# Multiplying by Z inside the recurrence for one unit, with heads kept on their row half, merged masks, diagonals on ScalarE and a new instruction order

## The chip, the cores and the metric

The kernel runs on one core of a Trainium2 chip, in float32. The metric is the device time of one launch in microseconds (us). Engines are named as the profile does: PE is TensorE's matmul, PEld its weight load, DVE is VectorE, ACT ScalarE, POOL GpSimd, SP SyncE. Before the change the median of three runs is 597.41 us (595.88 to 597.56).

## The reference

```python
# attention: B, H, S, D = 4, 8, 768, 48
k_n = k / (np.linalg.norm(k, axis=-1, keepdims=True) + 1e-06)
for t in range(S):
    y[:, :, t] = np.einsum('bhd,bhde->bhe', q[:, :, t], state)
    v_old = np.einsum('bhde,bhd->bhe', state, kt)
    state = state + bt * np.einsum('bhd,bhe->bhde', kt, vt - v_old)
# mixer: x is (4, 768, 384), U (768, 32), V (32, 768), w_ch1 (384, 1536), w_ch2 (1536, 384)
h = x.transpose(0, 2, 1) @ U @ V
u = x + h.transpose(0, 2, 1)
out = u + np.maximum(u @ w_ch1, 0.0) @ w_ch2
```

A delta-rule recurrence runs over 768 tokens for each of 32 pairs of batch and head. Its output goes, heads side by side, through a low-rank mixing of tokens and a two-layer network over channels.

## The kernel before

The recurrence is computed in chunks of 64 tokens. Within a chunk the sequential part is a triangular system, so the kernel forms the products of the keys with themselves, inverts a unit triangular matrix (called Z in what follows) and from then on needs only matmuls. A *unit* is half of one batch element: six chunks of all eight heads. There are eight units, two (n = 0, 1 for the first) per batch element b.

The eight heads stand on 128 partitions as two row halves of 64 (g), and within each half four heads, numbered by j and par. `QUADS` lists the four pairs (par, g). A matmul whose contraction lies on one half of the rows and whose output goes to one half of the columns uses one 64x64 quarter of PE's array.

For a unit the steps are:

- `load`: k, q, v, and z. The z load brings the odd heads of k a second time, onto the other row half (tile `kz`).
- `grams` and in it `turn` or `turn_blocks` (transposes of k and q into `kq`) and `products` (L700): k with k, and k with q. The k products' blocks of 32x32 on the diagonal are gathered by L710 and L713; the q products are masked by DVE (L731) into `qk`, one operation for each par.
- `blocks`: DVE transposes the diagonal blocks (L794), `norms` takes the norms and writes the coefficients on the diagonal of tile `xt` (L627), then forward substitution in pairs of DVE operations (L803, L809), and a transpose back (L816). `joins` (PE L860, L874, L900, L918) puts the small blocks together to Z, which lies in `pg`; `diagonals` copies the rest.
- `prepare`, once for each half of a unit (three chunks): keys times Z (L1023, copied by ACT L1042 over the transposed keys in `kq`) and values times Z (L1034, copied by ACT L1047 over the values `vn`).

`recur` then goes through the twelve chunks of a batch element, one after another:

- L1072: transposed keys with the state; L1085 (DVE): z is the values less that;
- L1100: keys with z, the increment of the state; L1111 (DVE): the state s is the old one plus that. The next chunk's L1072 needs it.
- `outputs`: L983 (queries with the state) and L997 (`qk` with z), copied by ACT L967 into tile X.

In every unit the heads with par = 1 sit, between these steps, on the other row half than the one they were loaded on: `g ^ par` in the code. It is for this that `kz` is loaded.

When all twelve chunks of a batch element are there, `front` does the low-rank token mixing (L1393, L1412, L1417, L1436), and `wide` and `narrow` do the channel network for 256 tokens at a time (L1497 with ReLU L1462, then L1617 with seven products in place of eight, gathered by DVE L1537). The last batch element goes through a like scheme for the first layer (L1296, L1305). The weights come as float64 and are turned into float32 on the chip: ACT L1198, then three DVE operations (L1212, L1219, L1226) for each of fourteen slices; u_sb and v_sb are the first two.

No engine picks its work by itself. All steps are generators that yield between instructions; a list written out in the kernel, `ORDER`, says for each of 2259 places which generator goes on, and each engine runs its instructions in the order in which they were emitted. The costs in `op(...)` are notes for a planner that made the list; in the kernel they change nothing. PSUM is shared by four pairs of banks (`pair`) and two banks of the mixer.

Of the kernel before, what the change touches and what calls it, by code (L numbers as in the profile page):

```python
# [12 lines left out]
ALU = mybir.AluOpType  # L13
# [14 lines left out]
def kernel(  # L28
# [116 lines left out]
    add_up b0 i0 f00: 590 628 635; add_up b0 i0 f03: 659 670 676; add_up b0 i1 f00: 795 820 825; add_up b0 i1 f03:  # L145
    840 846 849; add_up b0 i2 f00: 954 1014 1042; add_up b0 i2 f03: 1030 1053 1058; add_up b1 i0 f00: 1146 1147 1163;
    add_up b1 i0 f03: 1186 1188 1192; add_up b1 i1 f00: 1313 1315 1347; add_up b1 i1 f03: 1363 1364 1371; add_up b1
    i2 f00: 1482 1490 1493; add_up b1 i2 f03: 1543 1551 1561; add_up b2 i0 f00: 1688 1689 1692; add_up b2 i0 f03:
    1708 1721 1727; add_up b2 i1 f00: 1844 1845 1846; add_up b2 i1 f03: 1888 1889 1892; add_up b2 i2 f00: 2027 2051
    2056; add_up b2 i2 f03: 2046 2047 2053; add_up b3 i0 f00: 2183 2184 2189; add_up b3 i0 f03: 2187 2188 2190;  # L150
    add_up b3 i1 f00: 2205 2206 2208; add_up b3 i1 f03: 2203 2204 2207; add_up b3 i2 f00: 2226 2229 2230; add_up b3
    i2 f03: 2227 2228 2231; blocks n0: 67 71 72 73 76 78 79 80 84 85 88 95 100 101 102 106 107 109; blocks n1: 134
    151 155 160 162 169 192 196 200 208 209 212 220 222 226 232 233 235; blocks n2: 482 491 495 498 500 502 508 510
    511 513 516 519 521 522 528 529 530 537; blocks n3: 700 718 722 724 727 732 733 753 757 761 766 768 769 770 772
    774 778 784 787 791 792 798 799 811 812 814 815 819 824 831 847 848 851 854; blocks n4: 966 976 978 979 982 986
    988 997 1006 1020 1028 1029 1038 1048 1063 1072 1078 1082 1084 1094 1096 1106 1107 1108 1109 1111 1112 1113 1117
    1118 1121 1123 1125 1132; blocks n5: 1175 1190 1207 1210 1217 1219 1223 1224 1235 1236 1239 1246 1254 1258 1270
    1275 1279 1284 1285 1286 1290 1291 1294 1295 1298 1301 1302 1323 1324 1328 1331 1335 1336 1342; blocks n6: 1507
    1519 1531 1533 1542 1552 1559 1565 1570 1572 1574 1578 1579 1588 1591 1599 1606 1616 1628 1639 1640 1644 1645
    1649 1650 1654 1656 1660 1661 1663 1665 1667 1669 1677; blocks n7: 1670 1729 1732 1735 1742 1746 1754 1762 1768  # L160
    1776 1781 1782 1795 1797 1799 1805 1806 1810 1830 1832 1833 1835 1839 1847 1852 1857 1865 1868 1869 1871 1872
    1887 1890 1894; both f0: 2123; both f1: 2141; both f2: 2143; both f3: 2121; both f4: 2176; both f5: 2191;
    channels b0 i0 e0: 541 542; channels b0 i0 e1: 543 545; channels b0 i0 e2: 546 548; channels b0 i0 e3: 575 579;
    channels b0 i0 e4: 594 595; channels b0 i0 e5: 608 620; channels b0 i1 e0: 764 775; channels b0 i1 e1: 777 781;
    channels b0 i1 e2: 783 785; channels b0 i1 e3: 793 802; channels b0 i1 e4: 804 805; channels b0 i1 e5: 816 833;
    channels b0 i2 e0: 897 898; channels b0 i2 e1: 909 911; channels b0 i2 e2: 912 934; channels b0 i2 e3: 945 963;
    channels b0 i2 e4: 964 965; channels b0 i2 e5: 969 1002; channels b1 i0 e0: 1122 1137; channels b1 i0 e1: 1139
    1140; channels b1 i0 e2: 1141 1142; channels b1 i0 e3: 1145 1148; channels b1 i0 e4: 1149 1165; channels b1 i0
    e5: 1166 1167; channels b1 i1 e0: 1272 1304; channels b1 i1 e1: 1305 1307; channels b1 i1 e2: 1309 1310; channels
    b1 i1 e3: 1312 1314; channels b1 i1 e4: 1316 1333; channels b1 i1 e5: 1334 1350; channels b1 i2 e0: 1440 1441;  # L170
    channels b1 i2 e1: 1447 1449; channels b1 i2 e2: 1463 1464; channels b1 i2 e3: 1466 1499; channels b1 i2 e4: 1501
    1514; channels b1 i2 e5: 1515 1528; channels b2 i0 e0: 1668 1671; channels b2 i0 e1: 1672 1673; channels b2 i0
    e2: 1682 1684; channels b2 i0 e3: 1685 1686; channels b2 i0 e4: 1690 1699; channels b2 i0 e5: 1700 1701; channels
    b2 i1 e0: 1804 1808; channels b2 i1 e1: 1809 1812; channels b2 i1 e2: 1815 1827; channels b2 i1 e3: 1855 1858;
    channels b2 i1 e4: 1860 1861; channels b2 i1 e5: 1875 1877; channels b2 i2 e0: 1951 1961; channels b2 i2 e1: 1963
    1964; channels b2 i2 e2: 1966 1977; channels b2 i2 e3: 1984 1992; channels b2 i2 e4: 2002 2012; channels b2 i2
    e5: 2024 2034; copies f0: 2081 2091; copies f1: 2131 2135; copies f2: 2083 2092; copies f3: 2085 2109; copies f4:
    2155 2156; copies f5: 2149 2162; cut f0 k0 to0: 2116; cut f0 k0 to1: 2126; cut f0 k1 to1: 2114; cut f1 k0 to0:
    2144; cut f1 k0 to1: 2173; cut f1 k1 to1: 2178; cut f2 k0 to0: 2106; cut f2 k0 to1: 2172; cut f2 k1 to1: 2137;
    cut f3 k0 to0: 2134; cut f3 k0 to1: 2122; cut f3 k1 to1: 2138; cut f4 k0 to0: 2160; cut f4 k0 to1: 2177; cut f4  # L180
    k1 to1: 2193; cut f5 k0 to0: 2166; cut f5 k0 to1: 2192; cut f5 k1 to1: 2186; diagonals n0 h0: 189 190 191 213 214
    224; diagonals n0 h1: 167 168 172 178 181 194; diagonals n1 h0: 302 306 311 319 334 346; diagonals n1 h1: 286 297
    316 317 320 321; diagonals n2 h0: 572 573 574 588 593 611; diagonals n2 h1: 615 632 660 692 701 704; diagonals n3
    h0: 865 866 881 883 884 888; diagonals n3 h1: 858 859 860 861 869 900; diagonals n4 h0: 1161 1174 1203 1204 1213
    1216; diagonals n4 h1: 1155 1156 1157 1160 1195 1209; diagonals n5 h0: 1354 1362 1387 1392 1394 1396; diagonals
    n5 h1: 1359 1360 1365 1395 1405 1406; diagonals n6 h0: 1723 1726 1736 1758 1767 1772; diagonals n6 h1: 1710 1711
    1752 1785 1786 1792; diagonals n7 h0: 1900 1901 1903 1906 1909 1912; diagonals n7 h1: 1904 1910 1920 1927 1933
    1935; first f0: 2097; first f1: 2133; first f2: 2105; first f3: 2103; first f4: 2159; first f5: 2165; front b0
    i0: 487 496 504 505 526 535; front b0 i1: 556 567 607 625; front b0 i2: 626 639 662 671; front b1 i0: 1047 1057
    1066 1079 1101 1105; front b1 i1: 1225 1234 1241 1250; front b1 i2: 1344 1349 1404 1426; front b2 i0: 1576 1592  # L190
    1603 1605 1611 1620; front b2 i1: 1625 1641 1743 1745; front b2 i2: 1771 1783 1817 1834; front b3 i0: 2043 2044
    2049 2052 2055 2059; front b3 i1: 2061 2063 2064 2065; front b3 i2: 2069 2071 2074 2076; gather b0 i0 h0 c0
    finalFalse: 677; gather b0 i0 h0 c0 finalTrue: 681; gather b0 i0 h0 c1 finalTrue: 760 800; gather b0 i0 h1 c0
    finalFalse: 703; gather b0 i0 h1 c0 finalTrue: 748 974; gather b0 i0 h1 c1 finalFalse: 717; gather b0 i0 h1 c1
    finalTrue: 723; gather b0 i1 h0 c0 finalFalse: 850; gather b0 i1 h0 c0 finalTrue: 852; gather b0 i1 h0 c1
    finalTrue: 890 1205; gather b0 i1 h1 c0 finalFalse: 864; gather b0 i1 h1 c0 finalTrue: 882 1228; gather b0 i1 h1
    c1 finalFalse: 871; gather b0 i1 h1 c1 finalTrue: 879; gather b0 i2 h0 c0 finalFalse: 1041; gather b0 i2 h0 c0
    finalTrue: 1049; gather b0 i2 h0 c1 finalTrue: 1104 1242; gather b0 i2 h1 c0 finalFalse: 1074; gather b0 i2 h1 c0
    finalTrue: 1103 1287; gather b0 i2 h1 c1 finalFalse: 1080; gather b0 i2 h1 c1 finalTrue: 1089; gather b1 i0 h0 c0
    finalFalse: 1189; gather b1 i0 h0 c0 finalTrue: 1208; gather b1 i0 h0 c1 finalTrue: 1269 1643; gather b1 i0 h1 c0  # L200
    finalFalse: 1220; gather b1 i0 h1 c0 finalTrue: 1249 1268; gather b1 i0 h1 c1 finalFalse: 1226; gather b1 i0 h1
    c1 finalTrue: 1238; gather b1 i1 h0 c0 finalFalse: 1361; gather b1 i1 h0 c0 finalTrue: 1388; gather b1 i1 h0 c1
# [230 lines left out]
    def half(i, size=L):  # L433
        return slice(L * i, L * i + size)
# [1261 lines left out]
```

## Time and profile before

| | before |
|---|---|
| median of three runs | 597.41 us |
| profiled execution, its own time | 596.68 us |
| span, first to last instruction | 595.00 us |
| mean granted clock of PE | 0.940 |
| PE busy | 560.1 us (94%) |
| DVE busy | 409.8 us (69%) |
| ACT busy | 217.0 us (36%) |
| first L1497 | 116.03 us |
| start of L1085 in chunks 1, 6, 11 of the first batch element | 61.22, 88.04, 106.53 us |

Times within the execution are from the span's start. "Granted clock" is the share of TensorE's full clock that the throttle let through. A line such as L860 is a line of the kernel before; new lines of the changed kernel are called new. In the listings, "x24" counts passes: a float32 matmul of this kernel shows as two passes when its tile is 64x64 or 32x32 or its moving side is narrow, so twelve such matmuls are 24 passes.

### The profile page before, as it was taken

The numbers are of one execution on the slowest core, as the hardware profiler recorded it, in microseconds if no ns is written. First come the engines' busy times: TensorE is split into PE (matmuls) and PEld (weight loads), VectorE is DVE, ScalarE is ACT, GpSimd is POOL, SyncE is SP. The second block draws the span as 40 slices with busy tenths as digits, with TensorE's granted clock in tenths as the row PEclk, the third lists the DMA queues.
The fourth block names the chain that finished last, engine by engine and source line by source line (L and its number), as shares of the span: only waits on it lengthen the run. The fifth ranks groups of instructions, "written<-read, shape, count | busy, mean of one in ns | idle before, by whom it ended". The sixth has DMA issues, their size and how long they took to land.

```text
span 595.0 us, 23442 instructions
## 1 busy us (share of the span) xinstructions
PE 560.1 (94%) x10428; PEld 482.4 (81%) x10428; DVE 409.8 (69%) x1011; ACT 217.0 (36%) x442; POOL 133.3 (22%) x229
## 2 busy tenths in 40 slices
PE   4797987899999999999999999999999999999997
PEld 4696876688989987989889888898899778556997
DVE  3889767899999359999893389998973154122542
ACT  2558374436313442144234340234343321334000
POOL 8142133215041507312105143250110000000000
PEclk9657556999999999999999999999999999999999
DMA  9762656624041225510302035420201000000000
GB/s 141 152 154 72 216 116 146 140 70 70 3 95 22 46 42 91 99 47 17 75 2 41 11 54 93 105 58 15 68 6 37 3 2 15 26 0 1 26 28 28
DMA packets 89445, 36.23 MB, mean 61 GB/s; under 512 B 75456, under 2 KB 87104, under 8 KB 89344
## 3 DMA queue, kind: packets, MB, share of 16 engines
q1 hardware_dynamic: 80800, 24.69, 19.4%
q0 software_dynamic: 6944, 9.74, 8.2%
q8 instruction: 82, 1.34, 1.0%
q10 hardware_dynamic: 1600, 0.30, 0.3%
q14 instruction: 19, 0.16, 0.1%
HBM read 29.98 MB, written 4.72 MB: 58 GB/s over the span
## 4 chain that ended last, share of the span: by engine, by line
PE 90%; DVE 4%; issue 2%; ACT 2%; DMA 1%; SPq 0%; DVEq 0%; ACTq 0%
PE P L1617 29%; PE P L1497 25%; PE P L1296 7%; PE P L700 4%; PE P L1072 3%; PE P L983 2%; PE P L997 2%; PE P L672 2%; PE P L874 2%; PE P L1100 2%; PE P L1034 2%; PE P L1023 2%; PE P L860 2%; PE P L1412 2%; PE P L1436 1%
## 5 line engine op out<-in xcount | busy, mean ns | idle before, releaser
L1497 PE MATMUL P<-ut,w_sb 128*128 128x256 f32 x648 | 150.3, 385 | 0.9 <-ACT ut L1439 0.9
L1497 PEld LDWEIGHTS P<-ut,w_sb 128*128 128x128 f32 x648 | 119.8, 190 | 17.8 <-ACT ut L1439 1.1
L1617 PE MATMUL P<-w_sb,hs 128*128 128x192 f32 x540 | 95.8, 330 | 0.0
L1617 PEld LDWEIGHTS P<-w_sb,hs 128*128 128x128 f32 x540 | 87.4, 190 | 3.6 <-issue 1.8
L809 DVE TENSOR_TENSOR xt<-xt,prod 128x112 f32<-128x112 f32 (+21 forms) x200 | 64.6, 323 | 6.9
L803 DVE TENSOR_TENSOR prod<-gs,xt 128x112 f32<-128x112 f32 (+21 forms) x200 | 63.5, 318 | 3.6
L1537 DVE TENSOR_TENSOR X<-X,P 128x192 f32<-128x192 f32 x84 | 29.0, 348 | 49.6 <-PE P L1617 49.4
L1462 ACT ACTIVATE hs<-P 128x512 f32<-128x512 f32 x54 | 32.3, 598 | 80.0 <-PE P L1497 70.4
L967 ACT COPY X<-P 64x192 f32<-64x192 f32 x96 | 30.1, 313 | 60.7 <-PE P L997 59.6
L1617 PE MATMUL P<-w_sb,S 128*128 128x192 f32 x288 | 50.6, 330 | 0.0
L1617 PEld LDWEIGHTS P<-w_sb,S 128*128 128x128 f32 x288 | 46.6, 190 | 1.6 <-issue 1.2
L939 ACT COPY slot<-zz 32x384 f32<-32x384 f32 x64 | 32.2, 508 | 17.2 <-DVE zz L816 10.5
L555 POOL DMA_DIRECT2D slot<-in_v_dram x32 | 21.2, 665 | 66.9 <-DVE slot L747 33.4
L700 PE MATMUL P<-slot 48*64 48x64 f32 x1536 | 32.0, 235 | 4.4 <-ACT slot L687 3.7
L700 PEld LDWEIGHTS P<-slot 48*64 48x64 f32 x1536 | 28.9, 148 | 8.7 <-ACT slot L687 5.0
L1085 DVE TENSOR_TENSOR z<-slot,P 128x192 f32<-128x192 f32 x44 | 15.4, 350 | 29.2 <-PE P L1072 28.9
L946 POOL MEMSET slot<- 32x384 f32 x32 | 13.2, 413 | 96.0 <-PE P L900 52.2
L1296 PE MATMUL P<-slot,w_sb 128*128 128x384 f32 x96 | 33.2, 487 | 0.6 <-ACT slot L1365 0.6
L541 POOL DMA_DIRECT2D slot<-in_q_dram x40 | 24.6, 621 | 40.8 <-DVE slot L747 28.1
L541 POOL DMA_DIRECT2D slot<-in_k_dram x40 | 24.5, 620 | 35.5 <-DVE prod L803 18.6
L555 POOL DMA_DIRECT2D slot<-in_k_dram x44 | 29.5, 675 | 9.0 <-PE P L1100 8.7
L1305 DVE TENSOR_TENSOR slot<-slot,P 128x384 f32<-128x384 f32 x18 | 9.3, 551 | 32.4 <-PE P L1296 24.3
(153 smaller groups left out, 926.0 us busy)
## 6 DMA issues: line engine op xcount, KB each, us to landing
out_dram<-X SPq DMA_DIRECT2D x22, 192.0 KB, 2.6
w_sb<-in_moe_w_ch_dram SPq DMA_DIRECT2D x10, 384.0 KB, 5.2
slot<-in_k_dram SPq DMA_DIRECT2D x48, 72.0 KB, 3.4
slot<-in_k_dram POOLq DMA_DIRECT2D x44, 72.0 KB, 3.3
slot<-in_v_dram SPq DMA_DIRECT2D x32, 72.0 KB, 3.4
slot<-in_v_dram POOLq DMA_DIRECT2D x32, 72.0 KB, 3.6
X<-in_moe_w_ch_dram SPq DMA_DIRECT2D x6, 384.0 KB, 4.4
wide<-in_moe_w_ch_dram SPq DMA_DIRECT2D x6, 384.0 KB, 4.7
```

The costliest lines, as they stand in the source:

```text
L541: queue.dma_start(out=blocked(n)[quarter(y % 4), j, g, :, 0:w], in_=src[b, 4 * g + 2 * j + par, hf * UC * L : (hf + 1) * UC * L, BK * low ...
L555: queue.dma_start(out=t[half(1 - g if name == "z" else g), :, to, 0:D], in_=src[b, 4 * g + s, hf * UC * L : (hf + 1) * UC * L, :].rearrang ...
L700: nc.tensor.matmul(p_g[half(g ^ (par * i)), par, c], kq[rows, c, j, 0, half(g)], kq[rows, c, j, i, half(g)], start=True, stop=True,)
L803: nc.vector.tensor_tensor(out=prod, in0=gb[:, :, j : j + 1, j + 1 :].to_broadcast([128, split, m, w]), in1=xb[:, :, 0:m, j : j + 1].to_bro ...
L809: nc.vector.tensor_tensor(out=xb[:, :, 0:m, j + 1 :], in0=xb[:, :, 0:m, j + 1 :], in1=prod, op=ALU.subtract,)
L939: nc.scalar.copy(pg[quarter(i), :, at, :, a : a + BK], cut(zc, h)[quarter(i)].rearrange("p r (c j) t -> p r c j t", j=2),)
L967: nc.scalar.copy(x[half(c % 2), c // 2, 4 * D * g : 4 * D * (g + 1)].rearrange("p (j r d) -> p r j d", r=2, d=D), states(p_y)[half(g)],)
L1296: nc.tensor.matmul(to, w, t, start=start, stop=stop, skip_group_check=True)
L1462: nc.scalar.activation(hs[:, fs[0] : fs[1] + 1 : fs[1] - fs[0]], p_f, ACTF.Relu)
L1497: nc.tensor.matmul(p_f[:, x], w(x, t), ut[:, t], start=(t == 0), stop=(t == KT - 1))
L1537: nc.vector.tensor_tensor(out=to, in0=to, in1=p, op=ALU.add)
L1617: nc.tensor.matmul(to, of[0], of[1], start=of[2], stop=of[3], skip_group_check=True)
```

## The change

- Unit 1 (`DIRECT = (1,)`) has no preparation. Its keys and values stay without Z; in each of its six chunks the difference of values and keys times state is written back over the values (DVE), then multiplied by Z (eight matmuls, new L1107), and ACT copies the result to z (new L1117).
- Units 0 and 1 (`NATURAL = (0, 1)`) keep all heads on the row half on which they were loaded: the outputs of L700 (for q), L1072 and the preparation of unit 0 go to half g, and L1100 takes the keys themselves. Their z loads go (eight DMAs).
- In all units the q products are masked by one DVE operation over both par in place of two.
- In all units the coefficients go to the diagonal of `xt` by an ACT copy (new function `spread`) in place of the DVE copy L627; the substitution waits for it.
- `ORDER` is a new list, of 2247 places in place of 2259.

By engine PE has 48 matmuls fewer, DVE 24 operations fewer (16 masks, 8 diagonals), ACT 10 more (6 copies to z, 8 diagonals, less 4 of the preparation), SP and POOL 4 DMAs fewer each.

```diff
+    DIRECT = (1,)
+    NATURAL, ONCE = (0, 1), ()
...
+    def spread(n):
+        yield op("act", 0.2)
+        nc.scalar.copy(
+            out=xt.rearrange("p s t -> p (s t)")[:, 0 : BK * BK : BK + 1], in_=cp[:, n % 2]
+        )
+        emitted(("spread", n), 0.06)
...
-        nc.vector.tensor_copy(
-            out=xt.rearrange("p s t -> p (s t)")[:, 0 : BK * BK : BK + 1], in_=cp[:, n % 2]
-        )
+        begin(spread(n), 2)
...
-                        p_g[half(g ^ (par * i)), par, c],
+                        p_g[half(g ^ (par * i * (n not in NATURAL))), par, c],
...
-                for par in range(2):
-                    yield op("dve", dve(384), give=[("pair", x)] if par else ())
-                    nc.vector.tensor_tensor(
-                        out=qk[:, par, :, j],
-                        in0=p_g[:, par],
-                        in1=mask_u[:, None, :].to_broadcast([128, UC, L]),
-                        op=ALU.mult,
-                    )
+                yield op("dve", dve(768), give=[("pair", x)])
+                nc.vector.tensor_tensor(
+                    out=qk[:, :, :, j],
+                    in0=p_g,
+                    in1=mask_u[:, None, None, :].to_broadcast([128, 2, UC, L]),
+                    op=ALU.mult,
+                )
...
-                at = half(g ^ par)
+                at = half(g ^ par * (n not in NATURAL))
...
             yield need(("upper", n, h), ("diagonal", n, h), ("grams", n), ("scaled", n), *landed("k", n, 0), *landed("k", n))
+            if n in DIRECT:
+                emitted(("ready", n, h))
+                return
...
+            if direct:
+                xz = yield op("pe", 0.35 if n in NATURAL else 0.23, "Q", take="pair", words=32, flow=0.16)
+                p_z = pair(xz)[:, :, 0 : 2 * D]
+                for j, par, g in heads:
+                    nc.tensor.matmul(
+                        states(p_z)[half(g ^ par * (n not in NATURAL)), par, j],
+                        zt[half(g), par, cu, j],
+                        vn[half(g), cu, 2 * par + j],
+                        start=True,
+                        stop=True,
+                    )
+                yield need(("y", b, c - 3)) if c > 2 else []
+                yield op("act", act(192), give=[("pair", xz)], rush=True)
+                z = zs[c] = small.tile([128, 4, D], FP32, name="z", bufs=3)
+                nc.scalar.copy(z.rearrange("p (r j) d -> p r (j d)", r=2), p_z)
...
-                        kz[at, cu, j] if par else kn[at, cu, 2 * j, 0:D],
+                        kz[at, cu, j] if par and n not in NATURAL else kn[at, cu, 2 * j + par, 0:D],
...
-                if n or y:
+                if (n or y) and not (name == "z" and n in NATURAL):
```

More of the change, by code (lines that the diff above doesn't have):

```diff
@@ L798, in blocks @@
         nc.vector.tensor_tensor(out=gb, in0=gb, in1=by, op=ALU.mult)
+        yield need(("spread", n))
         for j in range(size - 1):
@@ L1072, in recur @@
                     nc.tensor.matmul(
-                        states(p_b)[half(g ^ par), par, j],
+                        states(p_b)[half(g ^ (0 if direct or n in NATURAL else par)), par, j],
                         kq[half(par, D), cu, j, 0, half(g)],
@@ L1081, in recur @@
                     begin(outputs(c, s_old), 2 if b == 0 else 60)
-                yield need(("y", b, c - 3)) if c > 2 else []
+                yield need(("y", b, c - 3)) if c > 2 and not direct else []
                 yield op("dve", dve(192), give=[("pair", xb)])
-                z = zs[c] = small.tile([128, 4, D], FP32, name="z", bufs=3)
+                z = vn[:, cu]
+                if not direct:
+                    z = zs[c] = small.tile([128, 4, D], FP32, name="z", bufs=3)
                 nc.vector.tensor_tensor(
```

421 lines of the change are left out of this document (211 added, 210 removed).

## The prediction

> **What bounds the kernel now.** I read the page's busy tenths first, to see where TensorE (PE) is not full; then the windows, for the granted clock in those stretches; then the chain of waits through the first 116 us; last the timeline of VectorE (DVE) and PE around one step of the recurrence, for prices.
>
> ```profile
> PE   4797987899999999999999999999999999999997
> ...
> DVE  3889767899999359999893389998973154122542
> ...
> PEclk9657556999999999999999999999999999999999
> ```
>
> A slice is 14.9 us. From the ninth slice on PE is full and its clock is full. Only the first eight slices, some 116 us, leave room: PE has gaps there and a clock near one half.
>
> ```profile
> 30.00:45.00 15.00, 14.40 (x338) 13.74 (x337) 13.11 (x36) 8.75 (x18) 6.52 (x10) 0.50 0.61 149
> 59.60:86.90 27.30, 24.71 (x796) 23.29 (x798) 19.20 (x35) 15.71 (x36) 5.44 (x10) 0.50 0.55 166
> 86.90:90.30 3.40, 1.67 (x104) 1.51 (x97) 1.45 (x3) 1.46 (x2) 2.02 (x4) 1.00 1.00 183
> 120.00:150.00 30.00, 29.34 (x923) 24.69 (x921) 29.70 (x55) 15.39 (x29) 10.79 (x18) 1.00 0.33 67
> ```
>
> Columns: window, its length, busy PE, weight loads, DVE, ACT and POOL, then granted clock, DMA share, GB/s. In 59.6 to 86.9 PE is busy 24.71 of 27.30 us at clock 0.50. From 120 on it is 98% busy at full clock.
>
> The first L1497 (the mixer's first large matmul) starts at 116.03. The order of instructions shows that both kernels have exactly the same matmuls from that point to the end (2180 of 64x64 tiles, 960 of 128x128, 768 of 32x32, 36 of 128x32), and that the 48 matmuls which go all stood ahead of it. So the change has to pay before 116.03, or through the order behind it.
>
> ```profile
> 82.75 0.92 ACT power L1198
> ...
> 84.25 1.53 PE P L1034 x48
> 85.78 1.29 PE P L1023 x48
> ...
> 87.99 1.73 issue
> ...
> 94.27 1.10 issue
> ```
>
> This is the chain of waits where the recurrence passes from unit 0 to unit 1. L1023 and L1034 are the preparation of unit 1 that goes. Two stretches of "issue" (PE has no visible wait) follow its dense matmuls.
>
> ```profile
> 84.04 0.34 DVE L1111 TENSOR_TENSOR s<-s,P 128x192 f32<-128x192 f32 x1
> ...
> 88.04 0.35 DVE L1085 TENSOR_TENSOR z<-slot,P 128x192 f32<-128x192 f32 x1
> 90.41 0.35 DVE L1111 TENSOR_TENSOR s<-s,P 128x192 f32<-128x192 f32 x1 [2.02 <-PE P L1100]
> 91.57 0.35 DVE L1085 TENSOR_TENSOR z<-slot,P 128x192 f32<-128x192 f32 x1 [0.80 <-PE P L1072]
> ...
> 92.74 0.35 DVE L1111 TENSOR_TENSOR s<-s,P 128x192 f32<-128x192 f32 x1 [0.35 <-PE P L1100]
> ```
>
> The recurrence in DVE's timeline. Unhindered, s to z takes 1.16 us (90.41 to 91.57) and z to s 1.17 (91.57 to 92.74). At chunk 6, the first of unit 1, they took 4.00 and 2.37.
>
> ```profile
> 20.58 1.56 PE L700 MATMUL P<-slot 48*64 48x64 f32 x48 [1.55 <-ACT slot L687]
> ...
> 37.13 1.47 PE L860 MATMUL P<-zz,hs 64*64 64x16 f32 x24
> ...
> 92.14 0.54 PE L1100 MATMUL P<-z,slot 64*48 64x48 f32 x16
> ```
>
> Two prices of a small matmul at half clock (each shows as two passes). L700 goes round all four 64x64 quarters of the array: 48 passes in 1.56 us, less one pass's own 0.3, is 27 ns a pass. L860 uses only the two quarters whose rows and columns are the same half: 24 passes in 1.47, less 0.26, is 53 ns. Twice the price. At full clock the starts are 14 ns (L1034, 55.4) and 29 ns (L860, 56.1) apart.
>
> **The change, part by part.** Sums are against the profiled execution: 596.68 us, span 595.00. The median of the runs is 597.41, 0.73 above it; the difference found is added to the median.
>
> *Unit 1's preparation goes.* Chunk 6 then waits for the state and no longer for L1023, L1034 and their copies L1042, L1047 (two of each, 0.80 and 0.64 us of ACT). s to z falls from 4.00 to 1.16: -2.85. z to s falls from 2.37 to 1.17, since the second half's L1034 and the 1.73 us of issue no longer stand between: -1.20. The stall at 94.27 (z to s 2.10 at chunk 8) may go with the dense matmuls, or not: 0 to -0.93; I take -0.9: the three other such stalls (58.0, 67.4, 88.0) stand inside or behind bursts of dense matmuls, and there are fewer of those.
>
> *Unit 1 multiplies by Z in every chunk.* A new step stands between z and the state's matmul: eight matmuls (new L1107) and an ACT copy (new L1117), six times. By the code row half equals column half in all eight, so only two quarters work: the L860 price, 15 starts of 53 ns and a pass of 0.30 are 1.10 us; then 0.31 of ACT (a 192-wide copy, L967) and about 0.1 of handing over: 1.5. Against it, L1100 now stands 0.22 behind L983 in PE's queue, and that is covered: 1.3. The bound below is four quarters (L997 starts are 23 ns apart at half clock): 0.64 in place of 1.10, so 0.85. The row nearest in tiles is L860, the nearest in shape L997; I take 1.2, near the first. At full clock, as from 100.6 on, 0.85. Five at 1.2 and one at 0.85, and 0.3 where L997 now stands ahead of the new matmul: +7.15 (bounds 5.1 and 8.5). Queued behind it are the state's L1100 and all later chunks, hence the front of the mixer.
>
> *Heads stay on their row half in units 0 and 1.* L700, L1072 and L1100 still go round four quarters. L997 (eight matmuls, twelve chunks) and unit 0's L1034 (48 matmuls) now use two. L997 costs 16 x 30 ns = 0.48 more at half clock. In chunks 1 to 5 it stands in a stretch where PE sets the pace (24.71 of 27.30): 0 to +2.4; PE's remaining 2.6 us of gaps cover about half: +1.2. L1034 costs 96 x 15 ns = 1.4 at full clock or 96 x 27 = 2.6 at half; it lies beside DVE's substitution of unit 1, which ends with L816 at 55.9, just ahead of the first state copy at 59.57: 0 to +2.6, taken +0.7. The eight loads of k that go (SP and POOL, about 0.65 us of issue and 72 KB each) are worth nothing by themselves: what waited for z loads does not show among the longest waits. If the DMA that they free did let weights arrive earlier, DVE would still be late for them, busy 13 of 15 us.
>
> *Masks in one step.* Two DVE operations of 0.53 us become one of 768 wide; by L1417 (768 wide, 0.95) four units' worth, i.e. two products in each of units 0 and 1, save 4 x 0.1. *Diagonals by ScalarE*: 0.20 us of L627 leaves DVE eight times; a 0.2 us ACT copy lies beside DVE's L798 (0.68). Both together -0.8 before the mixer if nothing else changed. But the new order puts both long weight operations of v_sb (L1212, L1219, 0.98 and 0.91) ahead of the first state copy and those of w_sb ahead of the first z. That costs up to 1.9: net -0.8 to +1.1, taken +0.3. For the other six units the two edits lie under a full PE: nothing.
>
> *The new order.* L860 of unit 1 stands behind chunk 0's state update and its products are spread over chunks 1 to 5 in smaller pieces. PE's gaps between 59.6 and 86.9 are 2.6 us (1.07 of them an issue stall at 67.4), the most that packing can win: 0 to -2.6, taken -1.8. The two turns of unit 2's k now stand together in chunk 10, and DVE's weight operations fill it as before; from the last L997 to L1497 the same work stands in another order, 0.1 less. Behind L1497 there are 142 changes of tile shape for 146; a group of six L1497 alone takes 1.49 us against 1.31 (a twelfth of 15.74), so a pair of changes costs near 0.2: -0.4. Short distances between z and s matmuls there are 29 against 27 of 65: nothing, +-1.
>
> Sum: -2.85 -1.2 -0.9 +7.15 +1.2 +0.7 +0.3 -1.8 -0.1 -0.4 = **+2.1 us**, so 599.5.
>
> **A rule weighed.** PE was 96% busy in 30 to 45 at clock 0.50, so being busy did not bring the full clock there; I therefore price by half clock until 100.6. The Trainium skill (TensorE: Matmul & The Clock Gate, section Part 1) says that about 3.4 us of sustained matmul activity lifts the clock to full. The trace does not bear that out for small tiles in this window. By that rule the packed stretch would run at full clock, which is the second rival below.
>
> **Rivals.**
> 1. *Faster*: the new step costs as four quarters do and the rest of the added passes stays under waits. Then +5.1 for the steps, nothing for L997, L1034 and DVE, and -2.6 for packing: -2.85 -1.2 -0.9 +5.1 -2.6 -0.1 -0.4 = -2.95, 594.5. It decides if passes of the new matmul start 23 ns apart or less at half clock. For it: DVE and PE both have gaps. Against: L860's 53 ns. Chance 0.27.
> 2. *No change*: the clock is full in the recurrence's second half. Six steps at 0.85 are 5.1, L997 costs 0.24 (+0.6 uncovered), L1034 +0.7: the sum with the other terms is -0.55, 596.9. For it: 86.9 to 90.3 was full. Against: that followed the preparation which goes. Chance 0.27, with all that lies within 0.3%.
> 3. *Slower still*: half clock lasts through chunk 10, where 12 turns (L672, 218 ns at half clock against 146) and 96 passes of L700 (27 against 15 ns) take 2.0 more: 601.5. It belongs to the slower side.
> 4. *Not what it says*: the z loads were hidden, so of that edit only the two-quarter price is left; this is in the sum.
>
> **How the numbers follow.** 0.3%, 1.8 us, is about what a measurement of this kernel can tell from no change. The forecast and the third rival together have 0.46, of which the forecast 0.36; its own range is 598 to 602. The range for all reaches from rival 1's 594.5, less 1 for the order behind L1497, to all upper bounds but packing, about 603.5: 593.5 to 603.5.
>
> **What would show it.** Right: first L1497 near 118.5 (116.03 + 2.5); new L1107 passes about 53 ns apart at half clock; z to s in chunks 6 to 10 near 2.4 us in place of 1.17; chunk 6's s to z near 1.2; no L1023 after 60 us; behind L1497 the same 479 us within 1. Wrong: L1497 ahead of 115, or passes of L997 in unit 0 still 23 ns apart, or a clock over 0.8 between 84 and 100, or a stretch behind L1497 that differs by over 1.5 us.

## The result, and the profile after

The changed kernel takes 601.42 us (median of eight runs, 599.39 to 604.55) against 597.48 for the kernel before in the same runs. The ratio is 1.0062, with a 95% interval of 1.0036 to 1.0088: slower by 2 to 5 us. A ratio, here and below, is estimated from all runs but one slow one of e9, so it is not quite that of the two medians. The forecast was 599.5 with a range of 593.5 to 603.5. The profiled execution is 601.46 us, its span 599.4.

Most lines move by the new code: L1085 (z) is now L1097, L1111 (s) L1138, L1072 is L1082, L1100 is L1127, L997 is L1003, L983 is L989, L1034 is L1043, L672 is L678, L700 is L706, L1219 (weights on DVE) is L1246, L1497 is L1524. L1107 and L1117 are the new Z step.

| profiled execution, us | before | after | |
|---|---|---|---|
| z of chunk 1 | 61.22 | 62.52 | +1.30 |
| from there to the state of chunk 5 | 22.82 | 19.37 | -3.45 |
| from there to z of chunk 6 | 4.00 | 1.33 | -2.67 |
| z of chunk 6 to z of chunk 11 | 18.49 | 25.30 | +6.81 |
| z of chunk 11 to the first L1524 (L1497) | 9.50 | 10.57 | +1.07 |
| **first L1524** | **116.03** | **119.09** | **+3.06** |
| from there to the end of the span | 478.95 | 480.35 | +1.40 |
| around the span | 1.70 | 2.02 | +0.32 |

The page's busy tenths of the changed kernel, with the granted clock:

```profile
PE   4697988899999999999999999999999999999997
...
DVE  3888858899999469999973269999981144323542
...
PEclk9756655999999999999999999999999999999999
```

The seventh slice (89.9 to 104.9 us) has a clock of one half; before, it was two thirds. The windows of the changed kernel (columns as in the prediction's listing of windows):

```profile
59.60:86.90 27.30, 25.24 (x794) 23.96 (x786) 19.95 (x37) 17.23 (x38) 7.50 (x13) 0.58 0.62 188
86.90:90.30 3.40, 2.97 (x76) 2.66 (x68) 1.66 (x4) 1.38 (x3) 0.95 (x2) 0.50 1.35 168
90.00:104.70 14.70, 12.04 (x244) 11.20 (x248) 11.72 (x19) 7.04 (x16) 5.59 (x9) 0.50 0.61 128
120.00:150.00 30.00, 29.61 (x860) 24.90 (x860) 28.30 (x54) 14.24 (x27) 9.90 (x17) 1.00 0.23 41
```

and the third of them in the kernel before:

```profile
90.00:104.70 14.70, 11.52 (x381) 10.22 (x377) 11.29 (x21) 7.19 (x15) 4.62 (x8) 0.65 0.62 150
```

In the same 14.7 us the changed kernel gets 244 passes done in place of 381, with PE busier than before. The full clock that 86.9 to 90.3 had is gone, and the final rise comes at 104.7 in place of 100.6.

The new step in the chain of waits, at chunk 6, the first of unit 1:

```profile
83.83 1.20 PE P L1107 x16
...
85.06 0.33 ACT z L1117
...
85.42 0.62 PE P L1127 x16
...
86.06 0.36 DVE s L1138
```

The same place in DVE's timeline:

```profile
81.89 0.35 DVE L1138 TENSOR_TENSOR s<-s,P 128x192 f32<-128x192 f32 x1 [0.72 <-PE P L1127]
83.22 0.35 DVE L1097 TENSOR_TENSOR slot<-slot,P 128x192 f32<-128x192 f32 x1 [0.98 <-PE P L1082]
...
86.06 0.35 DVE L1138 TENSOR_TENSOR s<-s,P 128x192 f32<-128x192 f32 x1 [1.02 <-PE P L1127]
87.29 0.35 DVE L1097 TENSOR_TENSOR slot<-slot,P 128x192 f32<-128x192 f32 x1 [0.87 <-PE P L1082]
```

From s to z chunk 6 now takes 1.33 us. Before, 4.00 us, DVE's timeline shows what ended that wait last:

```profile
85.51 0.56 DVE L1212 TENSOR_SCALAR w_sb<-X 128x768 int32<-128x768 int32 x1 [1.12 <-ACT X L1198]
86.10 0.96 DVE L1219 SCALAR_TENSOR_TENSOR w_sb<-hs,w_sb 128x768 int32<-128x768 int32 x1
87.09 1.06 DVE L1226 SCALAR_TENSOR_TENSOR w_sb<-hs,w_sb 128x768 uint16<-128x768 uint32 x1
88.04 0.35 DVE L1085 TENSOR_TENSOR z<-slot,P 128x192 f32<-128x192 f32 x1
```

PE was through with this chunk's L1072 at 87.29, behind the preparation, and z then stood behind a slice of weights in DVE's queue until 88.04. In the changed kernel the preparation is gone and the slice comes behind z.

From z to s chunk 6 takes 2.84. In chunks 7 and 9 that is 2.64 and 2.72, where an unhindered step took 1.17. In chunk 8 it is 3.82, because PE stands for 1.06 us ahead of L1127 (timeline):

```profile
92.76 0.32 ACT L1117 COPY z<-P 128x192 f32<-128x192 f32 x1 [1.72 <-PE P L1107]
93.10 0.64 ACT L973 COPY X<-P 64x192 f32<-64x192 f32 x2
...
94.20 0.57 PE L1127 MATMUL P<-z,slot 64*48 64x48 f32 x16 [1.06 <-ACT X L973]
```

z was ready at 93.08 and the copies that the profile names as what PE waits for ended at 93.74; in the last 0.45 us there is no visible wait. The last group of experiments shows what such stalls are.

The starts of L1107's passes lie 50 to 52 ns apart in chunks 7 to 9 and 27 to 30 ns at full clock (chunks 10 and 11). L1003 in units 0 and 1 went from 23 to 50 to 52 ns. Those are the prediction's 53 and 29 ns.

### The profile page after: what moved, and what is told of

Same layout as the page of the kernel before. It is cut to its first block, busy times and chain, and to the rows that moved or that the text cites. A ratio compares the mean times of both kernels' runs of the same rounds, so it can differ in the third digit from the quotient of the medians.

```text
span 599.4 us, 23253 instructions
## 1 busy us (share of the span) xinstructions
PE 565.6 (94%) x10332; PEld 488.9 (82%) x10332; DVE 409.1 (68%) x987; ACT 216.8 (36%) x452; POOL 131.0 (22%) x225
## 3 DMA queue, kind: packets, MB, share of 16 engines
q8 instruction: 81, 1.33, 0.9%
## 4 chain that ended last, share of the span: by engine, by line
PE 84%; DVE 8%; ACT 3%; issue 2%; DMA 1%; SPq 0%; POOL 0%; DVEq 0%; ACTq 0%
PE P L1644 27%; PE P L1524 22%; PE P L1323 7%; PE P L706 4%; PE P L1082 3%; PE P L1003 2%; PE P L1043 2%; DVE prod L809 2%; PE P L880 2%; DVE xt L815 2%; PE P L1127 2%; PE P L1032 2%; PE P L989 2%; PE P L866 2%; PE P L1439 1%
## 5 line engine op out<-in xcount | busy, mean ns | idle before, releaser
L1524 PE MATMUL P<-ut,w_sb 128*128 128x256 f32 x648 | 150.4, 385 | 0.9 <-ACT ut L1466 0.9
L1524 PEld LDWEIGHTS P<-ut,w_sb 128*128 128x128 f32 x648 | 119.9, 190 | 17.7 <-ACT ut L1466 1.1
L952 POOL MEMSET slot<- 32x384 f32 x32 | 13.2, 411 | 133.9 <-PE P L909 102.0
L945 ACT COPY slot<-zz 32x384 f32<-32x384 f32 x64 | 32.2, 508 | 16.4 <-DVE zz L822 9.2
L1097 DVE TENSOR_TENSOR z<-slot,P 128x192 f32<-128x192 f32 x38 | 13.3, 350 | 30.5 <-PE P L1082 30.2
L706 PEld LDWEIGHTS P<-slot 48*64 48x64 f32 x1536 | 28.7, 148 | 5.6 <-issue 3.1
L706 PE MATMUL P<-slot 48*64 48x64 f32 x1536 | 31.9, 235 | 1.1 <-issue 0.7
L1644 PE MATMUL P<-w_sb,slot 128*128 128x192 f32 x180 | 30.4, 327 | 0.9 <-DVE X L1564 0.9
L1138 DVE TENSOR_TENSOR s<-s,P 128x192 f32<-128x192 f32 x40 | 13.9, 348 | 24.9 <-PE P L1127 20.0
L1644 PEld LDWEIGHTS P<-w_sb,slot 128*128 128x128 f32 x180 | 29.3, 190 | 1.7 <-DVE X L1564 1.5
```

The costliest lines, as they stand in the source:

```text
L706: nc.tensor.matmul(p_g[half(g ^ (par * i * (n not in NATURAL))), par, c], kq[rows, c, j, 0, half(g)], kq[rows, c, j, i, half(g)], start=Tr ...
L945: nc.scalar.copy(pg[quarter(i), :, at, :, a : a + BK], cut(zc, h)[quarter(i)].rearrange("p r (c j) t -> p r c j t", j=2),)
L1524: nc.tensor.matmul(p_f[:, x], w(x, t), ut[:, t], start=(t == 0), stop=(t == KT - 1))
L1644: nc.tensor.matmul(to, of[0], of[1], start=of[2], stop=of[3], skip_group_check=True)
```

## The experiments

Theory A is the prediction's: the Z step and L1003 lose the time, by passes on two quarters at half clock. Theory B: the new order loses it and the parts are neutral. C (the clock), D and E (the supply of PE instructions) came up from the traces on the way. Head is the start of the first L1524 (L1497), rest is from there to the end of the span, both in the one profiled execution, whose time stands beside the median. It can lie off the median: e4's is its fastest run, e5's and e10's are their slowest. The kernel before ranged over 6 to 8 us beside each group of runs, so a difference of 1 or 2 us in one head or rest proves nothing by itself. "Edges" sums PE's stalls (over 0.06 us) at the edges of instruction blocks in the chain of waits, in head and rest; the last group of experiments explains them.

| run | median us | ratio to before (95%) | profiled us | head | rest | edges, head / rest |
|---|---|---|---|---|---|---|
| before | 597.48 | | 596.68 | 116.03 | 478.95 | 4.68 / 0.89 |
| after | 601.42 | 1.0062 (1.0036 to 1.0088) | 601.46 | 119.09 | 480.35 | 0.45 / 0.99 |
| e1_prepared | 610.31 | 1.0184 (1.0147 to 1.0221) | 608.55 | 121.83 | 484.84 | 0.84 / 3.71 |
| e2_crossed | 601.17 | 1.0048 (1.0025 to 1.0071) | 600.78 | 119.58 | 479.27 | 3.42 / 0.60 |
| e3_order | 610.35 | 1.0178 (1.0139 to 1.0217) | 610.24 | 121.73 | 486.42 | 5.53 / 5.03 |
| e4_small | 605.46 | 1.0096 (1.0058 to 1.0133) | 601.52 | 117.14 | 482.67 | 3.90 / 1.55 |
| e5_direct | 606.08 | 1.0114 (1.0073 to 1.0154) | 609.36 | 127.67 | 479.98 | 5.63 / 1.56 |
| e6_small_same_banks | 598.41 | 0.9995 (0.9965 to 1.0026) | 600.57 | 116.48 | 482.39 | 7.61 / 1.17 |
| e7_all_but_order | 608.19 | 1.0144 (1.0108 to 1.0181) | 608.08 | 122.23 | 484.14 | 0 / 1.60 |
| e8_fill | 614.66 | 1.0246 (1.0204 to 1.0288) | 615.57 | 127.33 | 486.21 | 6.49 / 4.71 |
| e9_fill_big | 613.66 | 1.0237 (1.0179 to 1.0294) | 609.52 | 120.48 | 487.04 | 0.67 / 5.59 |
| e10_after_pad56 | 608.79 | 1.0175 (1.0133 to 1.0217) | 613.11 | 122.61 | 488.51 | 5.23 / 5.11 |
| e11_after_pad192 | 612.39 | 1.0232 (1.0197 to 1.0267) | 612.33 | 125.95 | 484.39 | 4.07 / 4.69 |
| e12_before_pad64 | 600.31 | 1.0047 (1.0018 to 1.0076) | 600.29 | 116.73 | 481.85 | 7.17 / 1.89 |

The kernel before had medians of 598.0, 599.5, 598.4 and 598.2 beside the four groups of runs (e1 to e4, e5 to e8, e9, e10 to e12).

### Heads crossing again (e2)

```diff
-    NATURAL, ONCE = (0, 1), ()
+    NATURAL, ONCE = (), ()
```

with the eight places of the z loads put back into `ORDER` among the other early loads.

> The changed kernel with heads crossing to the other row half again in units 0 and 1 (NATURAL empty, its eight z loads back); unit 1 still multiplies by Z in the recurrence. Theory A: the Z step's 16 passes go from 53 to about 26 ns (1.20 to 0.65 us, five times: -2.7), L1003 from 0.85 to 0.43 us (-0.4 in each of five chunks on the path, -1 to -2 in chunks 1 to 5): 595 to 598. Theory B: 601 within 1. A third reading, that the z loads' 576 KB compete with the weights for the queues, gives 602 or more.

601.17 us, no difference from the change: theory B's number (601 within 1), not theory A's (595 to 598). The price itself was as theory A had it: L1107's passes start 25 ns apart in chunks 7 to 9, L1003's 23 to 25, and z of chunk 6 to z of chunk 11 takes 24.19 us in place of 25.30. What was won there was given back elsewhere: chunks 1 to 5 lost 1.0 us, with a PE stall of 0.91 at 73.73 that the change does not have there, and the front lost 0.9, with the clock at half from 109.9 to 113.3. So in these two traces keeping heads on their half costs about 1.1 us where it stands on the path, and nothing in the end. Stalls at block edges differ too: 3.42 us in this head, 0.45 in that of the change.

### Unit 1 prepared again, in the new order (e1, e3)

```diff
-    DIRECT = (1,)
+    DIRECT = ()
```

The twelve Z places of `recur b0` go. `prepare n1 h0` stands ahead of chunk 6, `prepare n1 h1` in chunks 7 and 8, where two copies of `outputs b0 c6` were moved ahead. e3 also has heads crossing again.

> The changed kernel with unit 1 prepared again as before the change (DIRECT empty): its six Z steps go, its L1030 and L1041-type matmuls come back in the gaps of chunks 6 to 8. Heads stay on their row half, masks, diagonals and the rest of the order stay. The changed kernel is 601.4 us, the one before 597.5. Theory A (the loss is the Z step's and L1003's passes on two quarters at half clock): six steps of about 1.5 us go, preparation costs some 4 to 5 back, so 597.5 to 600; z to s in chunks 7 to 9 falls from 2.6-3.8 to about 1.6. Theory B (the loss is the new order): no gain, 601 or more.

> Both edits undone (unit 1 prepared, heads crossing, z loads back), in the new order with merged masks and diagonals on ScalarE. Theory A: the order itself is neutral, 596 to 599. Theory B: the order makes the loss, 600 to 602.

Both 610, far above theory A's 597.5 to 600 and 596 to 599; theory B's "601 or more" allows e1, its 600 to 602 misses e3. Of the loss against the change, 4 to 6 us lie behind the head, where nothing was edited. e1 and e3 differ only in where the heads sit, and that again makes no difference. Two things were not held fixed: the later users of PSUM got other pairs of banks, and 192 PE instructions more stand ahead of the rest. The next runs show what each of these can do, so these two leave open what preparing unit 1 is worth in the new order.

### The small edits alone (e4, e6)

The kernel before, in its order, with the merged mask and `spread` (its place right behind each `norms`). In e4 the place of the second mask is dropped, in e6 it is kept as an empty one ahead of the merged mask:

```diff
+                yield op("dve", 0.0)
                 yield op("dve", dve(768), give=[("pair", x)])
```

> The kernel before, in its own order, with only the two small edits: one mask operation for the q products of both par, and the diagonal of xt by ScalarE (its place right behind the norms). Theory A: -0.8 to 0 against before's 597.5, as both lie beside other work. A rival: the hand-over from DVE to ACT and back stands on DVE's chain ahead of each substitution, +0.3 us in each of the two units that stand before the mixer: 598.

> The run with the two small edits again, but with the place at which the q products' banks come free kept, so that every later user gets the same pair of banks as in the kernel before. If the loss of that run (605.5) came from the shifted rotation of banks (its first L1524 waited behind a mask on DVE), this one keeps only what its recurrence showed, z of chunk 11 at 103.3 in place of 106.5: 595 to 597. If the loss comes from the ACT diagonal or the merged mask itself: 603 or more.

605.5 and 598.4, with the same operations. e4 lies above all its forecasts. The empty place decides when a pair of banks counts as free, hence which pair every later user gets. In e4 the pair that becomes the mixer's had last been used by a q product of unit 2. Its mask (here L740) stands behind much of the substitution in DVE's queue, and the first large matmul (here L1528) waits for it, as e4's chain of waits shows:

```profile
116.05 0.95 DVE slot L740
117.00 0.16 DVE prod L813
117.16 1.18 PE P L1528 x2
```

From z of chunk 11 to the first L1528 e4 takes 13.89 us, and e6 9.48. But e4's early recurrence nearly makes up for that in this trace (601.52 against e6's 600.57), so the 7 us between the medians are not seen in the traces, and that the banks make them is not shown.

With before's banks kept, the two small edits are worth nothing that can be measured (0.9995). z of chunk 11, 103.25 in e4, is 107.00 in e6, so the early recurrence that e4 showed did not come from the edits either, and the part of the expectation that built on it was wrong.

### The Z step alone, and the change without its order (e5, e7)

e5 is the kernel before, in its order, with `DIRECT = (1,)` only. e7 has the whole change except the order. In both the eight places of `prepare n1` go, two Z places stand right behind each z of unit 1, and pairs of banks are numbered so that everything behind the head gets the same pair as before.

> The kernel before, in its own order, with one part of the change alone: unit 1 multiplies by Z in the recurrence (its eight preparation places go, the two Z places stand right behind each z); heads cross as before, masks and diagonals are the old ones; the pairs of PSUM banks behind the head are the same as before's, place by place. Theory A: the terms of the prediction at the four-quarter price: -2.85 -1.2 -0.9 for what goes, against six Z steps of 0.85 (prediction's lower bound) to 1.15 (z to s was 2.3 to 2.5 in the crossed run in place of 1.17): +0.1 to +2 against before, 598 to 600. Theory B (only the order lost time): -1 or better, 597 or less.

> The whole change except its order: Z step, heads on their row half, masks, diagonals, in the order of the kernel before (Z places right behind each z, diagonals behind the norms), with before's banks behind the head. If the new order is worth the 1.8 us of packing that the prediction gave it, 602 to 604; if it is neutral, 601; if the order is what loses (theory B), 598 or less.

606.1 and 608.2: theory B falls, and theory A's 598 to 600 for e5 is missed by 6. By their ratios the Z step alone loses 6.8 us in the old order and all parts together 8.6. The change loses 3.7 by its ratio, so the new order, with the same operations as e7, wins back about 4.9, head and rest together. The forecast had given its packing 1.8. In e5 the saving of 2.85 us at chunk 6 does not come: from s to z still takes 4.24. DVE's timeline of e5 shows what is late next (L1145 is s, L1104 z, the three others one slice of weights):

```profile
86.65 0.34 DVE L1145 TENSOR_TENSOR s<-s,P 128x192 f32<-128x192 f32 x1
88.39 0.56 DVE L1246 TENSOR_SCALAR w_sb<-X 128x768 int32<-128x768 int32 x1 [1.40 <-ACT X L1232]
88.98 0.96 DVE L1253 SCALAR_TENSOR_TENSOR w_sb<-hs,w_sb 128x768 int32<-128x768 int32 x1
89.97 1.01 DVE L1260 SCALAR_TENSOR_TENSOR w_sb<-hs,w_sb 128x768 uint16<-128x768 uint32 x1
90.89 0.33 DVE L1104 TENSOR_TENSOR slot<-slot,P 128x192 f32<-128x192 f32 x1
```

In the old order z of chunk 6 stands behind a slice of weights that waits for ACT, as it did before the change. The new order puts the slices between the steps (the change's DVE timeline above has z at 83.22 right behind L1082). So the -2.85 is the order's as much as the Z step's. Both runs also have 192 PE instructions fewer than before, which the last group of runs bears on.

### Work to hold the clock up (e8, e9)

The profiler's clock changes lie on a grid of 3.41 us. I summed rows x columns x streamed columns of all passes in each window of that grid, in whole-array columns (L1524's passes of 256 columns start 216 ns apart, which makes some 4050 in a window). Up to 120 us, in the traces of all fourteen kernels, 236 of 237 half-clock windows that were followed by another had at most 1408, and 48 of 62 that were followed by a full one had more. 61 of 62 full windows that were followed by a fall had at most 1248, and 76 of 87 that stayed had more. So hardly a window above 1410 failed to bring the full clock. But 14 of the 62 rises came after less, down to 804, and 11 of the 87 windows that stayed had at most 1248, down to 960. Missing records do not explain these: the traces' counts of passes differ by just what the edits add or take. The sum goes with the clock, but it is not the whole rule. After the change the windows from 63.8 to 101.3 have 496 to 745.

e8 adds 24 groups of four 64x64 matmuls on four quarters (384 PE instructions), e9 adds 14 matmuls of one 128x128 tile and 256 columns (56 PE instructions), at spots of the recurrence, with results that nothing reads:

```diff
+    def fill(n):
+        x = next(iter(free["pair"]))
+        for _ in range(n):
+            nc.tensor.matmul(
+                pair(x)[:, 0, 0:256].rearrange("p (a n) -> p a n", a=2), ident,
+                ident[:, None, :].to_broadcast([128, 2, 128]), start=True, stop=True,
+            )
```

> The changed kernel with extra matmuls whose result nothing reads: groups of four 64x64 matmuls on four quarters, 128 columns each, at 22 spots of the recurrence between chunk 0 and chunk 10 (3 groups behind chunk 0's state, 2 ahead of chunk 6, else one each behind a matmul step). Theory C: the clock falls to half because the array's work (rows x columns x streamed columns, in whole-array columns) in a window of 3.41 us stays under about 1200, and rises after one above about 1410; the four rises and the falls of both kernels' traces agree with that. With the extra work the windows from 60 us on stay above, the clock stays full there, and the head gets shorter by some 5 to 12 us less 3 for the extra matmuls: 592 to 599. Rival: the gate looks at something else (being busy, or dense matmuls on 128x128 tiles), the clock stays half, and the extra passes cost 2 to 6 us: 603 to 607.

> The changed kernel with 14 extra matmuls whose result nothing reads, now of one 128x128 tile and 256 columns (four PE instructions each, 56 in all, where the fill before had 400): 3 behind chunk 0's state, then one in each chunk up to 10 and one more ahead of chunk 6. Each adds 512 whole-array columns to its window of 3.41 us. Theory C (rises above about 1410, falls below about 1250): the clock stays full from 57 us through most of the recurrence; a fill costs 0.43 us and a change of tile shape, mostly while PE waits for DVE or ACT in chunks 6 to 10; passes of L1107 go from 53 to 29 ns: head shorter by 3 to 8 us, 593 to 599. Theory D (PE's instruction supply bounds the dense stretch: a stall without visible wait ends 2.3 to 3 us after an instruction block of 16 KB starts to load): the clock is full but chunks 1 to 5 win nothing, stalls over 1 us stand there instead, and only chunks 6 to 10 win: 599 to 603. If the clock stays half: 605 to 610.

Added work did bring the full clock, though not by theory C's figure: the rises of e8 at 87.0 and 97.2 and of e9 at 86.2 follow windows of 1024, 1120 and 1094, where the changed kernel has 564 to 745. (e8's fills have 384 PE instructions, not the 400 of e9's expectation.) Both totals, 614.7 and 613.7, lie above everything that was expected. In e8 the clock is full from 56.3 to 69.9, 87.0 to 93.8 and 97.2 to 100.7, but the many small matmuls bring PE stalls of 2.59 us (at 66.09) and 1.86 (at 97.62) without a visible wait. In e9 the longest such stall in the recurrence is 0.60, so theory D is not what held it up, and the clock is full from 55.4 to 69.1 and from 86.2 to 133.9; windows of e9, then of the change:

```profile
69.10:86.20 17.10, 16.23 (x397) 13.44 (x397) 8.95 (x17) 7.85 (x19) 3.41 (x7) 0.50 0.33 102
86.20:104.70 18.50, 15.16 (x443) 11.87 (x446) 13.76 (x23) 8.95 (x19) 10.13 (x16) 1.00 0.88 166
```

```profile
69.10:86.20 17.10, 15.82 (x500) 14.76 (x496) 10.76 (x20) 9.76 (x25) 6.80 (x12) 0.50 0.56 168
86.20:104.70 18.50, 15.44 (x324) 14.28 (x328) 13.30 (x22) 8.11 (x17) 7.24 (x12) 0.50 0.75 134
```

Under the full clock 443 passes fit where 324 did, the steps from z to s fall to 2.04 (chunk 7) and 2.19 (chunk 9), and z of chunk 6 to z of chunk 11 takes 22.60 us in place of 25.30. So the half clock costs about 2.7 us there. It did not pay: where the clock stayed half (69.1 to 86.2) each of the three fills took 1.1 to 1.5 us of the chain, the head ends 1.4 later, and the rest, in which nothing was added, is 6.7 longer. That rest was the next question.

### Where the instruction blocks are cut (e10, e11, e12)

The page lists 81 transfers of the instruction queue with 1.33 MB, 16.4 KB each. 10332 passes and as many weight loads in 81 transfers are 255 each. The chains of the fourteen traces hold 44 PE stalls of over 0.9 us without a visible wait, and all 44 end 2.2 to 3.3 us after such a transfer starts (before: 2.6 to 2.7 for the stalls that end at 68.47, 89.72 and 95.37); of all moments, under a fifth lie so behind a transfer. I also counted PE's instructions in the traces (passes, weight loads and its few waits) up to the end of each stall. Divided by 256, all 44 counts leave the same rest, 193. So a block holds 256 PE instructions, and each of these stalls stands at the edge of one. L1127 of chunk 8 in the changed kernel is at such an edge too (94.20, 2.95 us after a transfer starts), as are all four stalls of 0.78 to 1.73 us in the head of the kernel before. The change takes 48 matmuls, 192 PE instructions, out ahead of the first L1524, and every block behind is cut elsewhere. To move only the cut, tiny matmuls were put ahead of everything, 14 and 48 of them in the change (56 and 192 PE instructions), 16 in the kernel before (64):

```diff
     with tc.manual_schedule():
+        for _ in range(14):
+            nc.tensor.matmul(P[0:32, 0, 0:8], ident[0:32, 0:32], ident[0:32, 0:8], start=True, stop=True)
```

> The changed kernel with 14 tiny matmuls (one 32x32 tile, 8 columns, result read by nobody) at the very start, where PE waits for the first load until about 6 us. They are 56 PE instructions, as many as the fill of 14 large matmuls had, so every later PE instruction lies at the same place in its instruction block of 256 as there. Theory E (the stage behind the first L1524 depends on where block boundaries fall in its bursts of small matmuls): from the first L1524 to the end 484 to 488 us in place of 480.4, as with the large fill (487.0), and 604 to 609 in all. Rival (the fills' own work or the clock made that stage longer): 480 within 1.5, 601 within 1.5 in all.

> The changed kernel with 48 such tiny matmuls at the start: 192 PE instructions, as many as the change takes away ahead of the first L1524, so that behind it the blocks are cut as in the kernel before. Theory E: that stage moves by more than 1.5 us against 480.4 (to 479 if before's cut is the better one for both, or up to 484 if the new order suits its own cut), and the total with it. Rival: 601 within 1.5, the shift of the cut is no term of the change.

> The kernel before with 16 such tiny matmuls at the start: 64 PE instructions, so that behind its head blocks of 256 are cut as in the changed kernel (192 fewer is 64 more). Theory E: slower by over 1.5 us, 599 to 604, with the stage behind the first L1497 longer than its 478.95. Rival: 597.5 to 598.5, no difference.

608.8, 612.4 and 600.3. The rest grows to 488.5, 484.4 and 481.9, by 8.2, 4.0 and 2.9 us, and the stalls at block edges in it by 4.1, 3.7 and 1.0. e10's rest is about as long as e9's, and the three longest stalls there stand at the same instructions, which shows that most of the large fill's loss behind the head came with the cut and not with its work. The stalls are not all of it (in e10 the clock also falls to half twice behind the head, at 135.3 and 159.2), and they do not simply add up: e6 has 7.6 us of them in a head as long as that of the kernel before.

In e10's chain of waits, a group of six transposes stops after five:

```profile
14.78 0.94 PE P L706 x45
15.72 0.70 PE P L678 x5
16.42 3.24 issue
19.65 0.49 PE P L678
```

The block's transfer starts at 16.75 and PE goes on 2.9 us later. That stall is about as long as the 3.5 us by which e10's head is late; three shorter ones follow in the head, and from z of chunk 6 to z of chunk 11 some 1.4 us are won back. In e12, behind the head:

```profile
131.89 0.89 PE P L860 x68
...
133.15 1.50 issue
134.65 0.21 PE P L900
...
134.96 2.79 PE P L1497 x12
```

and the kernel before at the same place, with no stall:

```profile
129.51 0.89 PE P L860 x68
...
130.87 2.79 PE P L1497 x12
```

Moving the cut alone makes the kernel before slower by a ratio of 1.0047 (1.0018 to 1.0076), nearly what the whole change does. It makes the change slower by 7 to 11 us, also where its cut behind the head is that of the kernel before (e11). Each of the two orders runs best, among the cuts that were tried, at its own.

No run beats the kernel before; e6 equals it.

## Why the prediction was right, step by step

**Head: +2.5 forecast, +3.06 measured, by terms that missed both ways.** That they nearly cancel is luck.

- *s to z of chunk 6*: -2.85 forecast, -2.67 measured. The size came, the reason was half right. In the kernel before z waited last for DVE's slice of weights and not for the preparation, so the saving needs the new order too (e5: nothing).
- *The Z step and L997 on two quarters*: right in mechanism and price (50 to 52 ns for 53). z to s over chunks 6 to 10 sums to 17.29 us against 10.90. The forecast's terms for it (-1.2, -0.9, five steps of 1.2, 0.3) make +4.2, and +6.4 came; 2.4 us a step was the sign named, 2.6 to 5.3 came. Two steps failed. In chunk 8 the terms make +0.3 (-0.9 and 1.2), and +1.72 came: the stall at 94.27 was to go with the dense matmuls, but it stood at a block edge, and now an edge lies at the first matmul of L1127 in that chunk. The other is the assumption that the clock is full from 100.6 on. It stayed half to 104.7, which was put aside as the third rival: the turns of unit 2's k in chunk 10 ran at half clock,

```profile
100.94 2.75 PE P L678 x12
103.69 1.32 PE P L706 x45
```

  where before only six of the turns' passes did (1.47 us) and all of L700's started 15 ns apart. z to s of chunk 10 took 5.27 for 3.52, +1.75 for 1.2. And the price, though right, is not shown to be what the whole change loses: e2 takes it away from the Z step, and the time stays 601.
- *Packing by the new order*: the mis-sized term. Forecast -1.8 with a bound of -2.6; chunks 1 to 5 got 3.45 us shorter in spite of L1003's double price (+1.2 in the forecast). The bound came from PE's gaps between 59.6 and 86.9, but work also left these chunks: they had 652 passes and have 584. Of the preparation that goes, 48 passes of L1023 stood there (at 82.46), which the forecast had not counted, and L918, L921 and L983 run elsewhere in part. e7 puts the whole order at about 4.9 us, head and rest together. The four largest stalls of before between 58 and 96 (at 58.0, 67.4, 88.0 and 94.3, 4.7 us), all at block edges, are down to one of 0.45. The prediction laid them to dense matmuls; where the edges fell was no part of it, so that much of the gain is luck too.
- *Unit 0's L1034 and DVE's order ahead of z of chunk 1*: +0.7 and +0.3 forecast, +1.30 measured together. L1043's 96 passes start 36 ns apart, 16 and 21 before.
- *Masks and diagonals*: nothing by themselves, which e6 confirms within 0.4%.
- *The last step, z of chunk 11 to the first L1524*: +0.75 forecast (0.85 less 0.1), +1.07 measured.

**Behind the head: -0.4 forecast, +1.4 measured in one profile; e2, with as many PE instructions, has +0.3.** The four fewer tile-shape changes cannot be seen in this. What the prediction lacked is that taking 192 PE instructions out cuts all later blocks elsewhere. In the profile of the change this does not make the +1.4: the stalls at block edges behind the head are 0.89 us before and 0.99 after. What makes it is open; it is within what one execution can differ from another.

**Rivals.** The first (four-quarter price) is excluded by the passes' distances. The second (full clock in the second half) did not happen. e9 brought that clock about and shows a price of about 2.7 us for its lack. The Trainium skill (TensorE: Matmul & The Clock Gate, section Part 1) makes sustained activity of about 3.4 us the condition. Here PE was 93% busy from 69.1 to 86.2 (15.82 of 17.10) at clock 0.50; its window length agrees with the grid, its condition does not for small tiles. The third rival (half clock through chunk 10) is what happened, beside the forecast.

## What to carry to other kernels

Price a small matmul by the quarters of the array that its tiles use and by the clock granted in that stretch: both were right to a few ns and could be read from the profile of before. Taking PE instructions out, or adding a few, can shift a tuned program by as much as the edit is meant to win, far behind the edit; put tiny matmuls ahead of the program to see how much of a result is that. When one part of a change is tried in an order written by hand, hold the rotation of PSUM banks and the count of PE instructions fixed, or the run measures those.

## What the hardware showed that was not expected

- *PE stalls on its instructions.* All 44 stalls of 0.9 to 3.2 us stand at the edge of a block of 256 PE instructions and end 2.2 to 3.3 us after a 16 KB block starts to load; the transfer itself takes 0.9 to 1.9. Most come in runs of small matmuls. The Trainium skill (Runtime: NRT & Kernel Launch, section Instruction fetch mechanics) gives blocks of 256 instructions and calls the cost of crossing them mostly hidden. The size agrees. "Mostly" holds by number (in the kernel before, 6 of 82 blocks show a stall in the chain), but the sum is 5.6 us there and 10.3 in e10, up to 3.24 at one edge.
- *The clock goes with the array's work, not with PE's being busy.* PE was 93% busy at half clock from 69.1 to 86.2. Of the windows of 3.41 us at half clock, 48 of the 49 with more than about 1410 whole-array columns (of some 4050 possible) were followed by the full clock, and 236 of the 250 with less were not. Of the windows at full clock, 61 of the 62 falls came after at most 1248, and 76 of the 77 with more stayed full. What decides below these figures is open.
